# The last output tile of an attention and MoE kernel leaves by column halves instead of row halves

## The chip, the cores and the metric

The kernel runs on one core of a Trainium2 chip. A core has five engines that run their own instruction streams: TensorE (PE in the profile; its weight loads are listed apart as PEld), VectorE (DVE), ScalarE (ACT), GpSimd (POOL) and SyncE (SP), which here only issues transfers. Transfers are issued from SP and from ACT, and their packets are moved by the core's 16 DMA engines. The metric is device time in microseconds (us), lower is better. A time is given as the median of several runs. A profile is one further execution with its own time.

## The reference, cut to what matters

For each of 8 batches and 8 heads of 64 the reference computes a linear attention over 576 positions, brings the heads side by side (512 columns), and sends all 4608 rows through two matrices with a squared ReLU between them:

```python
kv = np.einsum('bhsd,bhse->bhde', k_s, v)        # k_s: softmax over positions
attn = np.einsum('bhsd,bhde->bhse', q_s, kv)     # q_s: softmax over the head's 64
x = attn.transpose(0, 2, 1, 3).reshape(B * S, H * D)   # 4608 x 512
h = x @ w_in                                     # 512 x 2048
g = s * np.maximum(h, 0.0) ** 2 + b
return g @ w_out                                 # 2048 x 512
```

All inputs and the output are float32. The output has 4608 rows of 512 columns; a batch owns 576 consecutive rows.

## The kernel before

Float32 products are made from pairs of float32r parts (a high and a low part), three matmuls for each product. TensorE runs nearly without a gap from start to end, and the rest is arranged around it.

The rows are cut into nine blocks of 512. Blocks 0 to 7 are the first 512 rows of each batch. The ninth block is made of what is left: 64 rows of each of the eight batches. Within a block the 2048 hidden columns are taken in 16 steps of 128. Each step makes `h` in PSUM (line 998), squares and splits it on ScalarE and VectorE, and adds its share to four output tiles of 128 x 512 (line 1061). For the ninth block the hidden part is made earlier, spread over the time of block 7, and the output part is done at the very end by `final(j)`, j = 0 to 3 (line 984): each makes one output tile of 128 rows by 512 columns from 16 x 3 matmuls, one tile after the other. Each tile has a PSUM bank of its own. Tile j holds the 64 left rows of batch 2j in partitions 0 to 63, and those of batch 2j+1 in partitions 64 to 127.

`leave_last(j)` takes such a tile out. It copies the whole PSUM bank into a slice of one SBUF tile named `last` (line 1088), by VectorE for j = 2 and by ScalarE for the others, and then issues two transfers (line 1092). SP sends partitions 0 to 63 into the 64 rows of batch 2j, and ACT sends partitions 64 to 127 into the 64 rows of batch 2j+1. Each transfer has 64 rows of 2 KB, 128 KB in all. Both issues wait for the one copy.

The order of the instructions is found when the kernel is built, by a planner (`Order.run`): the work is a set of generators, each `yield Op(engine, cost, due, needs, ...)` asks for a place on an engine, and the code behind the yield is emitted when that place has been given. Each engine's stream is then fixed, and executes in that order. For j = 3 the requests of `leave_last` come after everything else that any engine does, so no planned work stands behind them. Semaphore waits between engines are put in by the framework, from the tiles that the instructions read and write. Behind the kernel's last instruction the framework puts a closing sequence (line 1248), in which SP waits for every transfer and all engines meet.

Of the kernel before, what the change touches and what calls it, by code (L numbers as in the profile page):

```python
# [25 lines left out]
def attention_moe(ctx: ExitStack, tc: tile.TileContext, q, k, v, w_in, w_out, s, b, out):  # L26
    nc = tc.nc
    B, H, S, D = q.shape
    DM, FF = w_in.shape
    DO = w_out.shape[1]  # L30
# [3 lines left out]
    NQ = 4  # L34
    LEFT = S - NQ * P
    NT = NQ + 1
    TB = NQ * P
# [950 lines left out]
    acc = {}  # L988
# [91 lines left out]
    def leave_last(j):  # L1080

        t = B * NFC + NFC * (j + 1)

        yield Op("DVE" if j == 2 else "ACT", 0.6, t, needs=[f"final {j}"])
        if not lasts:
            lasts.append(work.tile([P, AREA], F32, name="last", tag="area"))
        o = lasts[0][:, j * DO:(j + 1) * DO]
        (nc.vector.tensor_copy if j == 2 else nc.scalar.copy)(o, acc[B, j])  # L1088
        for i, (e, eng) in enumerate((("SP", nc.sync), ("ACT", nc.scalar))):
            yield Op(e, 0.1, t)  # L1090
            bb = 2 * j + i
            eng.dma_start(out[bb * S + TB:(bb + 1) * S, :], o[half[i]])
# [116 lines left out]
    with tc.manual_schedule(engines={E.PE, E.DVE, E.Activation, E.Pool, E.SP}):  # L1209
        order.run(  # L1210
            [others(), transfers(), scalars()] + [fetch(f) for f in range(NFE, NFC)]
            + [x for pr in range(NP // 2, NP) for x in reload(pr)]
            + [conv_w(0, slice(i, i + 1)) for i in range(2)] + [conv_w(f, slice(0, 2)) for f in range(1, NFC)]
            + [k_stream(u) for u in range(NP)] + [k_pair(pr) for pr in range(NP // 2, NP)]
            + [q_stream(u) for u in range(2 * NP)]
            + [kv_stream(pr) for pr in range(NP // 2)] + [kv_second(pr) for pr in range(NP // 2, NP)]
            + [step(t) for t in range(NSTEP - 2 * NFC)]
            + [x for pr in late for x in reload_late(pr)] + [k_late(pr) for pr in late]
            + [k_exps(u) for u in range(2 * NP, NU)] + [q_late(u) for u in range(2 * NP, NU)] + [between()] + [kv_late(pr) for pr in late] + [x_late(u) for u in range(2 * NP, NU)]
            + [leave(blk, j) for blk in range(B) for j in range(2)] + [leave_last(j) for j in range(NQ)] + [left_over()]  # L1220
            + operands() + [sums(i) for i in range(HP)] + [late_pe()] + [quadrant(p, n) for p in range(HP) for n in range(4)] + [final(j) for j in range(NQ)]
        )
# [30 lines left out]
```

## Time and profile before

| what | value |
|---|---|
| median of 3 runs | 859.88 us (859.0 to 860.23) |
| the profiled execution's own time | 860.12 us |
| its span, first to last instruction | 858.2 us |
| time outside the span (860.12 - 858.2) | 1.9 us |
| PE busy | 846.7 us, 99% of the span |
| DVE busy | 590.8 us, 69% |
| ACT busy | 435.7 us, 51% |
| the four final tiles, 192 matmuls of line 984 | 43.7 us busy |
| granted TensorE clock | 1.000 |

A busy share close to 100% says which engine carries most of the span, not what sets the very end of it. The end is read from the timeline and from the transfer views of the last microseconds. In a transfer view a packet is one piece that a DMA engine moves; a queue's row gives its packets, the MB, and the time that the packets took as a share of 16 engines over the window. A row of issues gives the count, the KB of each transfer and the microseconds from its issue until it has landed. q1 carries what SP issues, q10 what ACT issues.

### The profile page before, as it was taken

The numbers are of one execution on the slowest core, as the hardware profiler recorded it, in microseconds if no ns is written. First come the engines' busy times: TensorE is split into PE (matmuls) and PEld (weight loads), VectorE is DVE, ScalarE is ACT, GpSimd is POOL, SyncE is SP. The second block draws the span as 40 slices with busy tenths as digits, with TensorE's granted clock in tenths as the row PEclk, the third lists the DMA queues.
The fourth block names the chain that finished last, engine by engine and source line by source line (L and its number), as shares of the span: only waits on it lengthen the run. The fifth ranks groups of instructions, "written<-read, shape, count | busy, mean of one in ns | idle before, by whom it ended". The sixth has DMA issues, their size and how long they took to land.

```text
span 858.2 us, 11838 instructions
## 1 busy us (share of the span) xinstructions
PE 846.7 (99%) x4406; PEld 699.5 (82%) x4406; DVE 590.8 (69%) x922; ACT 435.7 (51%) x733; POOL 164.4 (19%) x184
## 2 busy tenths in 40 slices
PE   8899999999999999999999999999999999999997
PEld 6688888888888888888888888888888888888886
DVE  6999976778685857777587867685766587656300
ACT  5898744446364535454544454454336665555300
POOL 1000011111121110211020202120023436665000
PEclk9999999999999999999999999999999999999999
DMA  9994134334333324333424314421530110000100
GB/s 262 303 379 145 34 87 138 83 94 104 115 85 86 84 89 132 90 83 89 132 77 97 90 68 93 123 61 50 132 90 1 53 50 0 1 1 1 49 25 25
DMA packets 106573, 79.47 MB, mean 93 GB/s; under 512 B 56212, under 2 KB 100244, under 8 KB 106388
## 3 DMA queue, kind: packets, MB, share of 16 engines
q1 hardware_dynamic: 105364, 77.60, 32.4%
q10 hardware_dynamic: 1152, 1.11, 0.4%
q8 instruction: 35, 0.57, 0.3%
q14 instruction: 22, 0.18, 0.1%
HBM read 60.29 MB, written 18.40 MB: 92 GB/s over the span
## 4 chain that ended last, share of the span: by engine, by line
PE 94%; DMA 3%; DVE 1%; ACT 1%; issue 0%; SPq 0%; ACTq 0%
PE acc L1061 41%; PE h L998 35%; PE q L875 8%; PE last L984 5%; PE kv L311 2%; PE qa L875 1%; DMA st<-in_moe_w_out_dram 1%; DMA raw<-in_q_dram 1%; PE xp L690 1%; PE xq L690 1%; DMA area<-in_q_dram 1%; PE xp L454 0%; DVE low L232 0%; PE qT L444 0%; DVE w L239 0%
## 5 line engine op out<-in xcount | busy, mean ns | idle before, releaser
L998 PE MATMUL h<-x,w 128*128 128x512 f32 x1344 | 329.5, 391 | 0.8 <-DVE x L463 0.8
L1061 PE MATMUL acc<-w,gh 128*128 128x512 f32 x1024 | 317.7, 391 | 0.0
L998 PEld LDWEIGHTS h<-x,w 128*128 128x128 f32 x1344 | 250.1, 188 | 53.2 <-DVE x L463 1.4
L1061 PEld LDWEIGHTS acc<-w,gh 128*128 128x128 f32 x1024 | 190.9, 188 | 39.4
L1061 PE MATMUL acc<-w,gl 128*128 128x512 f32 x512 | 199.6, 390 | 0.1
L1023 ACT ACTIVATE r<-h 128x512 f32<-128x512 f32 x112 | 66.8, 596 | 170.8 <-PE h L998 168.3
L1036 DVE SCALAR_TENSOR_TENSOR r<-r,sb 128x512 f32<-128x512 f32 x106 | 84.5, 798 | 92.2 <-ACT r L1023 91.7
L1061 PEld LDWEIGHTS acc<-w,gl 128*128 128x128 f32 x512 | 96.1, 188 | 20.6 <-DVE gl L1040 0.5
L1038 ACT ACTIVATE gh<-r,sb 128x512 fp32r<-128x512 f32 x106 | 76.7, 724 | 53.8 <-DVE r L1036 52.9
L1040 DVE SCALAR_TENSOR_TENSOR gl<-r,sb,gh 128x512 fp32r<-128x512 f32 x106 | 83.2, 785 | 29.5 <-ACT gh L1038 28.6
L589 POOL TENSOR_TENSOR area<-area,qm 128x640 f32<-128x640 f32 x24 | 33.5, 1399 | 134.8 <-DVE qm L587 119.4
L606 POOL TENSOR_TENSOR qe<-qe,qr 128x640 f32<-128x640 f32 x24 | 32.3, 1348 | 75.9 <-DVE qr L602 41.1
L984 PE MATMUL last<-w 128*128 128x512 f32 x192 | 43.7, 389 | 0.0
L984 PEld LDWEIGHTS last<-w 128*128 128x128 f32 x192 | 36.1, 188 | 7.5
L670 POOL TENSOR_TENSOR spare<-kvf,spare 128x256 fp32r<-128x256 f32 x12 | 9.8, 820 | 129.9 <-issue 119.4
L696 ACT COPY y<-xp 64x320 f32<-64x320 f32 x48 | 20.2, 420 | 26.9 <-PE xp L690 26.5
L576 ACT ACTIVATE area<-area 128x640 f32<-128x640 f32 x24 | 17.6, 737 | 18.7 <-DVE area L538 18.7
L578 POOL MEMSET area<- 64x128 f32 x24 | 4.8, 200 | 116.2 <-issue 92.4
L958 DVE SCALAR_TENSOR_TENSOR gl<-r,sb,gh 128x512 fp32r<-128x512 f32 x16 | 13.7, 855 | 17.1 <-ACT gh L953 17.1
L700 DVE TENSOR_TENSOR y<-xp,y 64x320 f32<-64x320 f32 x48 | 23.4, 488 | 2.7 <-ACT y L696 1.7
L1088 DVE COPY last<-last 128x512 f32<-128x512 f32 x1 | 0.7, 692 | 34.6 <-PE last L984 34.6
L311 PEld LDWEIGHTS kv<-area 128*64 128x64 f32 x600 | 18.7, 137 | 5.1 <-issue 3.3
(190 smaller groups left out, 1073.4 us busy)
## 6 DMA issues: line engine op xcount, KB each, us to landing
st<-in_moe_w_in_dram SPq DMA_DIRECT2D x16, 512.0 KB, 8.3
st<-in_moe_w_out_dram SPq DMA_DIRECT2D x16, 512.0 KB, 9.0
out_dram<-o SPq DMA_DIRECT2D x16, 512.0 KB, 2.6
turned<-area SPq DMA_DIRECT2D x24, 320.0 KB, 2.3
qT<-turned SPq DMA_DIRECT2D x48, 160.0 KB, 3.1
area<-in_q_dram SPq DMA_DIRECT2D x14, 512.0 KB, 5.4
area<-in_k_dram SPq DMA_DIRECT2D x14, 512.0 KB, 4.3
area<-in_v_dram SPq DMA_DIRECT2D x56, 128.0 KB, 5.0
```

What stands on the lines that cost most here:

```text
L311: nc.tensor.matmul(kv[h * D:(h + 1) * D, i], kt[:, i, h, n], vt(2 * i + h, n), start=(n == 0), stop=(n == NT - 1))
L589: nc.gpsimd.tensor_tensor(out=qt, in0=qt, in1=bc(qm, [P, 2, NT, D]), op=ALU.subtract)
L606: nc.gpsimd.tensor_tensor(out=qe_, in0=qe_, in1=qr, op=ALU.mult)
L700: nc.vector.tensor_tensor(out=y[half[h], at], in0=parts[h][a][half[h]], in1=y[half[h], at], op=ALU.add)
L875: nc.tensor.matmul(BANK[where], w(a)[:, c * P:(c + 1) * P], xs[b_][:, c], start=k in (0, 1, 3) and n == 0, stop=n == 5, skip_group_check=True)
L984: nc.tensor.matmul(t_, g[:, js], w_, start=(f == 0 and i == 0), stop=(f == NFC - 1 and i == 2))
L998: nc.tensor.matmul(hp_, w[:, j, c, :], x[:, c, :], start=(c == 0 and i == 0), stop=(c == NP - 1 and i == 2))
L1023: nc.scalar.activation(r, hp_, AF.Relu)
L1036: nc.vector.scalar_tensor_tensor(out=r, in0=r, scalar=s_col, in1=r, op0=ALU.mult, op1=ALU.mult)
L1038: nc.scalar.activation(gh, r, AF.Identity, bias=b_col)
L1040: nc.vector.scalar_tensor_tensor(out=gl, in0=r, scalar=b_col, in1=gh.bitcast(F32), op0=ALU.add, op1=ALU.subtract)
L1061: nc.tensor.matmul(acc[blk, j // 2][:, j % 2], g[:, js], w_, start=(f == 0 and i == 0), stop=(f == NFC - 1 and i == 2))
```

## The change

Only tile j = 3, the last one, is treated in another way. Its bank is read by two engines, each for one half of the columns and all 128 partitions: ScalarE copies columns 0 to 255 and ACT sends them; VectorE copies columns 256 to 511 and SP sends them. The two transfers still carry 128 KB each, now as 128 rows of 1 KB. The destination of each is a view of the output with three dimensions, 2 batches by 64 rows by 256 columns, and the source is 128 partitions by 256 columns. The code emits ScalarE's copy, ACT's issue, VectorE's copy and SP's issue, in this order. Tiles 0 to 2 leave as before.

```diff
         o = lasts[0][:, j * DO:(j + 1) * DO]
+        if j == NQ - 1:
+            rows = out.rearrange("(b s) e -> b s e", b=B)[2 * j:2 * j + 2, TB:S]
+            for e, eng, copy, es in (
+                ("ACT", nc.scalar, nc.scalar.copy, slice(0, DO // 2)), ("SP", nc.sync, nc.vector.tensor_copy, slice(DO // 2, DO))
+            ):
+                copy(o[:, es], acc[B, j][:, es])
+                yield Op(e, 0.1, t)
+                eng.dma_start(rows[:, :, es], o[:, es])
+            return
         (nc.vector.tensor_copy if j == 2 else nc.scalar.copy)(o, acc[B, j])
         for i, (e, eng) in enumerate((("SP", nc.sync), ("ACT", nc.scalar))):
```

## The prediction

> **What bounds the kernel now.** I read the page first, for the span and the chain of waits that ended last, and then the last microseconds.
>
> ```profile
> span 858.2 us, 11838 instructions
> PE 846.7 (99%) x4406; PEld 699.5 (82%) x4406; DVE 590.8 (69%) x922; ACT 435.7 (51%) x733; POOL 164.4 (19%) x184
> PE 94%; DMA 3%; DVE 1%; ACT 1%; issue 0%; SPq 0%; ACTq 0%
> ```
>
> TensorE carries the span, and the change doesn't touch its work. What can move is only what follows the last matmul. The chain in order of time from 853 us on (start, length, what), and the timeline of the same window, show that piece:
>
> ```profile
> 852.97 0.69 PE last L984 x3
> 853.66 0.02 issue
> 853.68 0.58 ACT last L1088
> ```
>
> ```profile
> 853.68 0.58 ACT L1088 COPY last<-last 128x512 f32<-128x512 f32 x1 [21.17 <-PE last L984]
> 854.29 0.47 SPq L1092 DMA_DIRECT2D out_dram<-last  x1
> 854.30 0.50 ACTq L1092 DMA_DIRECT2D out_dram<-last  x1
> ```
>
> The last matmul ends at 853.66, the copy runs from 853.68 to 854.26, and both transfers are issued 0.03 later. No engine computes after that; SP's waits show what the closing sequence waits for:
>
> ```profile
> SPq L1248 <- DMA out_dram<-last: 2.1, 2, 1.8
> ```
>
> So the end is set by the later of the two landings. The transfer view of the window 854.2 to 858.2 (40 slices of 0.1 us in its first row) shows both:
>
> ```profile
> DMA  0000000000007999495998400000000000000000
> GB/s 0 0 0 0 0 0 0 0 0 0 0 0 184 246 184 266 82 225 123 349 471 328 164 0 0 0 0 0 0 0 0 0 0 0 0 0 0 0 0 0
> DMA packets 160, 0.26 MB, mean 66 GB/s; under 512 B 32, under 2 KB 32, under 8 KB 160
> q1 hardware_dynamic: 80, 0.13, 16.3%
> q10 hardware_dynamic: 80, 0.13, 8.6%
> out_dram<-last SPq DMA_DIRECT2D x1, 128.0 KB, 2.3
> ```
>
> In this window ACT's transfer stands without a landing time; the window 843.5 to 846.2, with the same pair for the tile before, has it:
>
> ```profile
> out_dram<-last ACTq DMA_DIRECT2D x1, 128.0 KB, 2.6
> ```
>
> Packets run from slice 12, 855.4, so 1.1 us after the issue, to slice 22, about 856.5. The later landing is ACT's: 854.30 + 2.6 = 856.9, which is 0.4 after the last packets. From there to the end of the span are 858.2 - 856.9 = 1.3 us of closing. The tail is then 0.6 copy and hop, 1.1 start, 1.1 packets, 0.4 report, 1.3 closing.
>
> The same view tells how a transfer is shared out. 160 packets with 32 under 512 B are 2 x 64 rows of 2 KB and 2 x 16 small packets, one report from each of 16 engines: a transfer whose outermost dimension counts 64 uses all 16. Packet times: q10 took 8.6% of 16 x 4.0 us = 5.5 us for 64 rows, 86 ns for 2 KB on one engine; q1 16.3%, 10.4 us, 163 ns.
>
> **The change, part by part.** *The copies.* Copies of half the width stand in the groups by form, for other PSUM tiles:
>
> ```profile
> L696 ACT COPY y<-xq 64x256 f32<-64x256 f32 x48 | 17.6, 367 | 0.9
> L700 DVE TENSOR_TENSOR y<-xq,y 64x256 f32<-64x256 f32 x48 | 20.3, 422 | 1.0
> L1088 DVE COPY last<-last 128x512 f32<-128x512 f32 x1 | 0.7, 692 | 34.6 <-PE last L984 34.6
> ```
>
> These have 64 partitions where the new copies have 128; 128x512 takes 0.58 on ACT, so partitions are not what a copy's time goes by, and 0.37 is my value for ACT. For DVE 0.42 is the nearest row, and 692 ns for twice the width bounds it above. ACT's half is therefore copied at 853.68 + 0.37 = 854.05 and issued at 854.08, 0.2 earlier than now.
>
> No row shows two engines reading one bank at the same time. If VectorE starts with ScalarE, it ends at 853.68 + 0.42 = 854.10; if it is made to wait for ScalarE's read, at 854.08 + 0.42 = 854.50, and SP's issue moves to 854.53, 0.24 later than now. I take the wait, since the two copies name the same tile and the code emits ScalarE's first. The Trainium skill, PSUM — Partial Sum Buffer, section on bank collisions, says that two engines on one bank and quadrant at once, reads included, are an error and have to be ordered by a semaphore; by it the second number holds, and no run here shows it. Behind VectorE's copy nothing is queued but the closing sequence, and only SP's issue waits for it.
>
> *The issues.* One on each of SP and ACT as before, 0.47 and 0.50 us, none moved past another. The change adds one DVE copy and takes no transfer away.
>
> *The transfers* are the large term. They keep 128 KB each, but get 128 rows of 1 KB, and their destination's outermost dimension counts 2 (the batches) where it counted 64. The trace has no transfer with 2 there. The rows on either side are the 64 of above (16 reports, all engines) and the one-row loads of `s` and `b`, outermost count 1:
>
> ```profile
> sb<-in_moe_s_dram SPq DMA_DIRECT2D x1, 0.0 KB
> sb<-in_moe_b_dram SPq DMA_DIRECT2D x1, 0.0 KB
> ```
>
> In the view of the whole span these are the only two rows with no landing time. I read that as reports missing: a landing is found from a transfer's reports, and a one-row transfer has no work for sixteen engines. So a transfer can run on fewer, and its shape decides. A count of 2 is far nearer to 1 than to 64, and I take it that such a transfer is dealt out in two shares, one for each batch, to two engines.
>
> The Trainium skill, DMA: Bandwidth & Descriptors, section "Why a DMA increments its semaphore by 16 and not by 1", has this as a rule: the number of engines is the largest up to 16 that divides the slowest dimension of both sides, and a hardware queue takes the lowest-numbered ones. Here that is the common divisor of 2 and 128, two engines, the same two for both queues; the 16 reports for 64 rows agree with it, and by it the sum is the one below.
>
> The price of a 1 KB row on one engine: rows of 1280 B from SBUF to DRAM, alone on the engines, stand in the window 133.7 to 136.0:
>
> ```profile
> DMA packets 272, 0.33 MB, mean 142 GB/s; under 512 B 16, under 2 KB 272, under 8 KB 272
> q1 hardware_dynamic: 272, 0.33, 41.1%
> ```
>
> 41.1% of 16 x 2.3 us is 15.1 us for 256 rows (and 16 reports), 59 ns each; by bytes 47 ns for 1 KB. The 86 ns for 2 KB give 43, the 163 ns of q1 give 82. I take 47: those rows are the nearest in size and, as here, come from all 128 partitions.
>
> *The sum.* ACT issues at 854.08; first packets 1.1 later, 855.2. Each of the two engines moves 64 rows of ACT's and 64 of SP's, if both queues use the same two: 128 x 0.047 = 6.0 us, to 861.2. SP's rows come from 854.53 + 1.1 = 855.6 on, long before ACT's 64 (3.0 us) are through, so the wait of VectorE's copy costs nothing: ACT's packets hide it. Without that cover it would cost up to 0.4. Then 0.4 for the report and 1.3 closing: the span ends at 862.9, 4.7 later than 858.2. The profiled execution would take 860.12 + 4.7 = 864.8; it lies 0.24 above the median of the runs, 859.88, so I predict 864.6. All times below are on the median's basis. At 43 ns the packets take 5.5 us (864.1), at 59 ns 7.6 us (866.2).
>
> **The rivals.**
>
> *Sixteen engines after all.* The mechanism is that the rows are dealt by the 128 source partitions. Then the packets are as short as now: 128 rows of 1 KB on 16 engines are 8 x 47 = 0.4 us for each transfer. ACT's half lands near 854.08 + 2.3 to 2.6 = 856.4 to 856.7, SP's at 854.53 + 2.3 to 2.6 = 856.8 to 857.1, against 856.9 now: -0.1 to +0.2 if VectorE waits, and about -0.2 if both copies run together. The time is 859.9, no slower than before. For it speaks that every transfer of 64 or 128 rows in this trace uses all engines; against it the one-row loads. This one decides if the outermost count of one side doesn't limit the shares. It also holds the case that the change doesn't do what it says: the copies then run one after the other, and what ACT's half gains SP's half loses.
>
> *Two engines, but another two for each queue.* SP's half starts at 855.6 and takes 64 x 0.047 = 3.0 us: 858.6, landed 859.0, span 860.3, +2.1: 862.0. For it: no row shows which engines a transfer of few shares gets. Against it: in the last pair now each queue has 16 reports, so the queues have no engines of their own.
>
> *Two engines at q1's rate.* SP's rows now take 163 ns for 2 KB, and ACT's 86. If the slow rate belongs to the destination or to writes that come first, all rows run at 82 ns: 855.2 + 10.5 + 0.4 + 1.3 = 867.4, +9.2: 869.1. For it: the 163 ns stand beside the 86 ns in one window and on the same engines. Against it: 256 rows of 1280 B ran at 59 ns from the same SBUF side.
>
> **How the numbers follow.** Two shared engines at 43 to 59 ns: 0.67, with a range of its own from 864.0 to 866.2. Sixteen engines: 0.17. Two engines for each queue apart: 0.08. The slow rate: 0.06. The remaining 0.02 is drift of the runs. A measurement of this kernel can tell about 0.2% from no change, 1.7 us, so the sixteen-engine case is "same" and the three others are slower: 0.81. Faster by 1.7 us has no mechanism: the only gain that the rows allow is 0.2 us. I give it 0.02, same 0.17. The range runs from 861.9 (queues apart) to 869.1 (the slow rate) and leaves out 0.19.
>
> **What would show it.** In the last window of the profile after: 260 packets (256 rows and 2 x 2 reports) confirm two engines, 288 refute them. The busy digits of the DMA row should stand at 1 (2 of 16 is 0.125) for some 6 us at about 43 GB/s; 3 us, or a digit of 2, is the rival with queues apart. Digits as high as now, with the end near 858.2, refute the forecast. The ACT copy should take 0.37, with its issue at 854.08; the DVE copy should start about 0.4 after ScalarE's, or together with it if reads are not ordered. SP's closing wait for the last transfer should grow from 1.8 us to between 6 and 7. Everything up to 853.66 should stand within 0.2 us of now; if not, the difference doesn't come from the tail.

## The result and the profile after

The kernel after takes 864.85 us (median of 6 runs, 864.28 to 866.22) beside 859.75 us before (6 runs, 859.0 to 860.23): 5.1 us slower, a ratio of 1.0061 with a 95% interval of 1.0048 to 1.0074. The forecast was 864.6, slower.

The page's first line and the timeline of the last microseconds, as they stand after the change:

```profile
span 863.0 us, 11839 instructions
```

```profile
853.23 0.37 ACT L1093 COPY last<-last 128x256 f32<-128x256 f32 x1 [21.17 <-PE last L984]
853.63 1.08 ACTq L1095 DMA_DIRECT2D out_dram<-last  x1
853.63 0.42 DVE L1093 COPY last<-last 128x256 f32<-128x256 f32 x1 [10.59 <-ACT last L1093]
854.08 0.60 SPq L1095 DMA_DIRECT2D out_dram<-last  x1
```

The two copies don't run together: VectorE is released by ScalarE's copy and starts when that has ended. ACT's issue comes 0.4 us after the start of the copy, earlier than the 0.6 before the change; SP's comes 0.85 after it. The issue itself now occupies ACT for 1.08 us where it took 0.50.

From the start of the last copy to the end of the span it was 858.2 - 853.68 = 4.5 us before and is 863.0 - 853.23 = 9.8 us now. This stretch, called the tail below, holds the whole loss: 5.2 us in the profile, 5.1 in the medians. (The two spans differ by 4.8 us only, because the last copy started 0.45 us earlier in the profile after.) The transfer view of the window 854 to 863 (40 slices of 0.225 us), and SP's waits, show where it goes:

```profile
DMA  0000111111110111120111111111111100000000
DMA packets 260, 0.26 MB, mean 29 GB/s; under 512 B 4, under 2 KB 260, under 8 KB 260
q10 hardware_dynamic: 130, 0.13, 5.2%
q1 hardware_dynamic: 130, 0.13, 4.4%
```

```profile
SPq L1257 <- DMA out_dram<-last: 7.0, 1, 7.0
```

260 packets are 256 rows of 1 KB and only 4 reports, two for each transfer, where 64-row transfers had 16 each. The busy digit is 1 nearly throughout the 6.5 us in which rows move, 854.9 to 861.4: about an eighth of the engines. The packets' time is 9.6% of 16 x 9 us, 13.8 us, or 6.9 us on each of two engines, which fills that stretch (the times of successive packets overlap a little).

These figures alone would also fit a pair of engines for each queue, used one pair after the other. The window 858.3 to 858.8, in which both queues move rows, tells the two apart:

```profile
DMA packets 24, 0.02 MB, mean 49 GB/s; under 512 B 0, under 2 KB 24, under 8 KB 24
q1 hardware_dynamic: 12, 0.01, 6.9%
q10 hardware_dynamic: 12, 0.01, 6.9%
```

Each queue has half of the rows, and together they keep 13.8% of the 16 engines busy, where ACT's queue alone had 14.4% in the window 857.0 to 857.4 and SP's alone 14.0% in 859.5 to 860.2. Two pairs at that pace would have shown twice as much. So two engines, the same for both queues, moved everything, and SP waited 7.0 us for the last landing.

### The profile page after: what moved, and what is told of

The parts are those of the page before. It is cut to its first block, busy times and chain, and to the rows that moved or that the text cites. A ratio compares the mean times of both kernels' runs of the same rounds, so it can differ in the third digit from the quotient of the medians.

```text
span 863.0 us, 11839 instructions
## 1 busy us (share of the span) xinstructions
PE 846.6 (98%) x4406; PEld 700.0 (81%) x4406; DVE 590.9 (68%) x923; ACT 435.4 (50%) x733; POOL 164.3 (19%) x184
## 4 chain that ended last, share of the span: by engine, by line
PE 96%; DMA 1%; ACT 1%; DVE 1%; SPq 0%; ACTq 0%; issue 0%; DVEq 0%
PE acc L1061 41%; PE h L998 35%; PE q L875 8%; PE last L984 5%; PE kv L311 2%; PE qa L875 1%; PE xp L690 1%; PE xq L690 1%; DMA area<-in_q_dram 1%; PE xp L454 1%; PE kT L342 1%; DMA area<-in_v_dram 0%; PE qT L444 0%; SPq L297 0%; PE kn L355 0%; PE unused L1210 0%
```

## Experiments

Tails are read as above, from the start of the last copy to the end of the span; the expectations count from the last matmul, which ends some 0.03 us before. The time that stands beside a run's is that of the kernel before, measured with it. Where no interval stands, the profiled execution is the only run, and its tail decides, not its time.

### The same rows to a destination of one dimension

```diff
-                eng.dma_start(rows[:, :, es], o[:, es])
+                eng.dma_start(out[2 * j * S + TB:2 * j * S + TB + P, es], o[:, es])
```

> The kernel after, but each of the two transfers of the last tile goes to 128 consecutive rows of the output (rows 0 to 127 from the first left row of batch 6) instead of 64 rows of each of two batches: the destination's outermost dimension counts 128 instead of 2, the copies, the 128 rows of 1 KB, the queues and the bytes are the same. Its second half therefore lands in the wrong rows: it leaves out the left rows of batch 7 and overwrites the first rows of that batch. Theory (the outermost count of 2 confines each transfer to two DMA engines): sixteen engines again, 288 packets in the last window, from the last matmul to the end of the span 4.2 to 4.8 us as before the change (4.6) and not 9.8, time 859.3 to 860.3. Rival (rows of 1 KB, column halves with a stride, or the second copy are what is slow): the tail stays near 9.8 us and the time near 864.8.

859.32 us beside 859.52, ratio 0.9997 (0.9988 to 1.0007). Timeline, and transfer view of the window 853.4 to 857.4:

```profile
853.49 0.37 ACT L1093 COPY last<-last 128x256 f32<-128x256 f32 x1 [21.17 <-PE last L984]
853.89 0.37 ACTq L1095 DMA_DIRECT2D out_dram<-last  x1
854.35 0.34 SPq L1095 DMA_DIRECT2D out_dram<-last  x1
```

```profile
core 0 of [0], span 857.4 us
DMA  0000000000000289968998200000000000000000
DMA packets 288, 0.26 MB, mean 66 GB/s; under 512 B 32, under 2 KB 288, under 8 KB 288
```

The loss is gone with nothing changed but where the rows go. The same copies, the same wait of VectorE, the same 256 rows of 1 KB: 32 reports instead of 4, digits of 8 and 9, and all rows moved in 1.0 us where it took 6.5. The rival with 1 KB rows, the column stride or the second copy as the cause falls. The tail of 3.9 us is even below the 4.2 expected, and 0.6 below that of the kernel before: the issues take 0.34 to 0.37 us and the first packet follows 0.9 us after its issue, where the 64-row transfers of before took 0.47 to 0.50 and 1.1.

### Four transfers, one for each batch and half

```diff
-                yield Op(e, 0.1, t)
-                eng.dma_start(rows[:, :, es], o[:, es])
+                for i in range(2):
+                    yield Op(e, 0.1, t)
+                    eng.dma_start(rows[i, :, es], o[half[i], es])
```

> The kernel after, but each engine sends its column half in two transfers, one for each batch: 64 rows of 1 KB each, the output complete and right. Theory (outermost count): each of the four uses 16 engines, 320 packets in the last window. ACT issues 0.4 and about 0.9 us after the last matmul, SP 0.9 and about 1.4 after it; the last lands 2.3 to 2.6 later, 1.3 closing: tail 5.0 to 5.4 us, time 860.1 to 860.7. Rival (1 KB rows or column halves): the rows are the same, so the tail stays near 9.8 and the time near 864.8.

859.73 us beside 859.52, ratio 1.0 (0.999 to 1.0009). In the window 852 to 862:

```profile
DMA packets 321, 0.27 MB, mean 27 GB/s; under 512 B 64, under 2 KB 320, under 8 KB 320
```

256 rows and 4 x 16 reports (and one instruction fetch behind the end). The copy starts at 852.47 and the span is 857.2: a tail of 4.7, a little under the expected 5.0 to 5.4, and the time is below the expected 860.1 to 860.7 as well. So the very same rows reach the very same places in the time of the kernel before when the batch is not a dimension of the transfer.

### The two parts of the change apart

Only the copies: both engines copy a half, then the tile leaves as before.

```diff
+        if j == NQ - 1:
+            rows = out.rearrange("(b s) e -> b s e", b=B)[2 * j:2 * j + 2, TB:S]
+            nc.scalar.copy(o[:, 0:DO // 2], acc[B, j][:, 0:DO // 2])
+            nc.vector.tensor_copy(o[:, DO // 2:DO], acc[B, j][:, DO // 2:DO])
+            for i, (e, eng) in enumerate((("SP", nc.sync), ("ACT", nc.scalar))):
+                yield Op(e, 0.1, t)
+                eng.dma_start(rows[i], o[half[i]])
+            return
```

> Only the copies of the change: ScalarE and VectorE copy a column half each, and then the tile leaves in row halves of 64 x 2 KB, by SP and ACT as before. Theory: the copies run one after the other (0.38 and 0.42 us), both issues come 0.9 us after the last matmul where they came 0.65 before, tail 4.8 to 4.9 against 4.6 us: within the noise of the time. Rival (the second copy's wait is a main cost): the tail grows by more than 1 us.

Only the sends: one copy of the whole tile by ScalarE, then the two transfers of the change.

```diff
-                copy(o[:, es], acc[B, j][:, es])
+                if e == "ACT":
+                    copy(o, acc[B, j])
```

> Only the sends of the change: ScalarE copies the whole tile as before (0.58 us), then ACT and SP send the column halves to the destination with outermost count 2. Theory: both issues come 0.65 us after the last matmul, 260 packets, the tail is the 9.8 us of the change and 0.2 more for ACT's later issue: 9.9 to 10.2. If one transfer's rows wait until the other's have been given out, whichever queue is first, the second queue's first packet comes some 3 us after its issue here too; if the queues interleave when they are issued together, both start about 1.1 to 1.8 after it and the end is the same. Rival (the copies): tail 4.6.

The timeline of the copies alone, then that of the sends alone:

```profile
852.36 0.37 ACT L1090 COPY last<-last 128x256 f32<-128x256 f32 x1 [21.17 <-PE last L984]
852.76 0.42 DVE L1091 COPY last<-last 128x256 f32<-128x256 f32 x1 [10.59 <-ACT last L1090]
853.22 0.47 SPq L1094 DMA_DIRECT2D out_dram<-last  x1
```

```profile
853.69 0.59 ACT L1094 COPY last<-last 128x512 f32<-128x512 f32 x1 [21.17 <-PE last L984]
854.30 0.60 SPq L1096 DMA_DIRECT2D out_dram<-last  x1
854.31 1.33 ACTq L1096 DMA_DIRECT2D out_dram<-last  x1
```

The copies alone: span 857.1, tail 4.7, 0.2 more than before, which is their coming one after the other (its one run took 858.88 us, 0.3 below the fastest of the 19 runs of the kernel before beside it, so its time shows no cost). The sends alone: span 864.0, tail 10.3 and 865.82 us, the whole loss and 0.5 more, where 0.2 was expected for ACT's later issue. Rows began 1.2 us after the first issue in both kernels, so of the 0.5 some 0.2 is that first issue's later time (0.6 against 0.4 after the start of the copy), and the rest lies in the packets. Here SP issued first, by 0.01 us, and its rows came first: in the window 853.6 to 857.4 all 56 packets are SP's, so ACT's first row moved more than 3.0 us after its issue. Which queue comes late is not a matter of the queue or of VectorE's wait.

### Sixty-two rows, and sixty

The kernel before, with each queue's 64 rows of the last tile cut in two transfers, 62 and 2 rows, or 60 and 4:

```diff
-            eng.dma_start(out[bb * S + TB:(bb + 1) * S, :], o[half[i]])
+            cut = 62 if j == NQ - 1 else LEFT
+            eng.dma_start(out[bb * S + TB:bb * S + TB + cut, :], o[i * D:i * D + cut])
+            if cut < LEFT:
+                yield Op(e, 0.1, t)
+                eng.dma_start(out[bb * S + TB + cut:(bb + 1) * S, :], o[i * D + cut:(i + 1) * D])
```

> The kernel before (one copy by ScalarE, row halves of 2 KB rows by SP and ACT), but for the last tile each queue sends 62 of its 64 rows first and the other 2 rows in a transfer of their own. Theory, made sharper (a transfer is dealt over the largest number of engines up to 16 that divides its outermost count on both sides): 62 = 2 x 31 gives two engines, 31 rows of 2 KB on each for each queue at 86 ns: 2.7 us for one queue, 5.3 to 5.8 for both, and the tail is 8.5 to 9.5 us; 136 packets in the last window (124 rows + 4 rows + 4 x 2 reports); time 863.5 to 864.7. Rival (only a small outermost count confines, a count of 62 still spreads over all engines with uneven shares): the tail is that of before and 0.5 to 1.0 more for the second issues, 5.1 to 5.6; time 860 to 860.6.

> The same with 60 rows and 4 rows instead of 62 and 2. Theory (largest divisor up to 16): 60 gives 15 engines and 4 gives 4: 166 packets in the last window (128 rows, 2 x 15 and 2 x 4 reports), tail 5.1 to 5.8 us, the second issues being all that is added to before. Rival (any transfer that is not a multiple of 16 falls to few engines, or a second small transfer in each queue is itself the cost): the tail is that of the 62 rows, above 8 us.

62 rows: 865.09 us beside 859.47, ratio 1.0064 (1.0049 to 1.008). 60 rows: 859.52 in its one run. The transfer views of the window 852 to 862, first for 62, then for 60:

```profile
DMA  0000000000200101111010111111111111000000
DMA packets 136, 0.26 MB, mean 26 GB/s; under 512 B 8, under 2 KB 8, under 8 KB 136
q1 hardware_dynamic: 68, 0.13, 4.6%
```

```profile
DMA  0000000000497771000000010000000000000000
q1 hardware_dynamic: 83, 0.13, 6.1%
q10 hardware_dynamic: 83, 0.13, 3.5%
```

These two runs decide what the engines are counted by. With 62 rows a queue has 64 data packets and 4 reports, which fit 2 from the 62 rows and 2 from the 2 rows. With 60 it has 64 and 19, which fit 15 and 4. With two rows fewer in a transfer of whole 2 KB rows, without a third dimension, the span grows from 858.2 to 863.2; with two fewer again it is 857.6. It isn't the third dimension, a small count or a second small transfer: what fits every count of reports is the largest divisor up to 16 of the outermost count. The Trainium skill, DMA: Bandwidth & Descriptors, section "Why a DMA increments its semaphore by 16 and not by 1", states this rule, the largest number up to 16 that divides the slowest dimension of both sides; the reports here agree with it at 64 (16), 62 (2), 60 (15), 4 (4) and 2 (2).

The tails missed the expected figures both ways: 863.2 - 853.12 = 10.1 for 62 rows (8.5 to 9.5 expected, and 863.5 to 864.7 for the time: the digits of 0 show gaps in which not even two engines were busy), and 857.6 - 853.10 = 4.5 for 60 (5.1 to 5.8 expected: the second issues, about 0.3 us each, cost nothing).

### Only ACT's half on two engines

SP's half goes in two transfers of 64 rows, ACT's as in the change:

```diff
-                yield Op(e, 0.1, t)
-                eng.dma_start(rows[:, :, es], o[:, es])
+                for i in range(2 if e == "SP" else 0):
+                    yield Op(e, 0.1, t)
+                    eng.dma_start(rows[i, :, es], o[half[i], es])
+                if e == "ACT":
+                    yield Op(e, 0.1, t)
+                    eng.dma_start(rows[:, :, es], o[:, es])
```

> The kernel after, but only ACT's half goes to the destination with outermost count 2; SP sends its column half in two transfers of 64 rows of 1 KB, one for each batch, which by the earlier runs use all 16 engines. Question: why SP's first packet came 3.6 us after its issue in the kernel after (1.1 to 1.2 us elsewhere). Theory G (the rows of all queues are handed out one transfer after another, so a transfer whose two engines are full holds up the next, even where that one's engines are idle): SP's first packet comes 2.5 us or more after its issue. Theory E (only the two engines are full): SP's first packet, on one of the 14 idle engines, comes 1.0 to 1.6 us after its issue. Under both the tail is set by ACT's transfer or by the shares of SP's rows on the two engines: 7.8 to 9.0 us after the last matmul, against 4.6 before and 9.8 after; packets 130 on ACT's queue, 160 on SP's.

The question behind it: in the kernel after, SP issues at 854.08, and in the window 853.2 to 857.65 the transfer view has packets of ACT's queue and none of SP's:

```profile
DMA packets 94, 0.10 MB, mean 22 GB/s; under 512 B 0, under 2 KB 94, under 8 KB 94
q10 hardware_dynamic: 94, 0.10, 8.2%
```

So SP's first row moved 3.6 us after its issue. In the mixed kernel SP issues at 854.66, and its rows are there in the window 853.7 to 856.2:

```profile
854.66 1.11 SPq L1096 DMA_DIRECT2D out_dram<-last  x2
```

```profile
q1 hardware_dynamic: 8, 0.01, 5.8%
q10 hardware_dynamic: 28, 0.03, 4.1%
```

They came within 1.5 us while ACT's two engines were full, so a confined transfer doesn't hold up all others; theory G falls. The tail is 861.4 - 853.80 = 7.6, just under the expected 7.8 (863.27 us in one run). But E isn't enough either: if the two engines only took turns between the queues, SP's rows would have mixed with ACT's from the start in the kernel after. They do mix once they have begun, 12 and 12 in the half microsecond shown in the section on the result. What puts the start of a second transfer for the same two engines 3 us behind stays open.

### One half alone, and one queue for both

> The kernel after without SP's transfer: the right half of the last tile's columns is copied and not sent (it is left out of the output). ACT's transfer of 128 rows of 1 KB to the destination with outermost count 2 is alone. Question: in the kernel after, the first 2.5 us of ACT's rows came at 62 ns a row on each engine, later rows at 42. If the slow beginning belongs to a transfer's own start: 64 rows on each engine take 3.5 to 4.0 us, tail 6.9 to 7.4 us after the last matmul. If it comes from SP's transfer, issued 0.45 us later, or from its handing out: 64 x 42 to 47 ns, 2.7 to 3.0 us, tail 6.1 to 6.4 us. Packets in the last window: 130. If the rows were on sixteen engines: tail below 4.

> The kernel after, but SP issues both column halves, ScalarE's first; ACT only copies. Question: whether the two queues' sharing of two engines costs or spares anything. If the two engines' total work is all that counts (256 rows of 1 KB on two engines): the tail is that of the change, 9.3 to 10.2 us. If the two queues had engines of their own in part, the tail would be above 10.5. If the late start of the second queue (3.6 us after its issue) were a loss, one queue would do without it and end at 64 + 64 rows x 47 ns, tail 9.0 to 9.3.

```diff
+                if e == "SP":
+                    return
                 yield Op(e, 0.1, t)
                 eng.dma_start(rows[:, :, es], o[:, es])
```

```diff
-                yield Op(e, 0.1, t)
-                eng.dma_start(rows[:, :, es], o[:, es])
+                yield Op("SP", 0.1, t)
+                nc.sync.dma_start(rows[:, :, es], o[:, es])
```

Transfer views, window 852 to 862, of the half alone and then of the one queue:

```profile
DMA  0000000000001111111111111000000010000000
GB/s 0 0 0 0 0 0 0 0 0 0 0 8 25 37 45 25 41 37 16 37 49 49 49 45 49 12 0 0 0 0 0 0 33 0 0 0 0 0 0 0
```

```profile
DMA  0000000000010111111111111111111111110000
q1 hardware_dynamic: 260, 0.26, 8.4%
```

The half alone has a tail of 859.9 - 853.34 = 6.6 us (861.73 us in one run), between the two bands that were expected. Its rows start slowly with no second transfer there: some 30 GB/s over the first 2 us, 49 GB/s after (two engines at 42 ns for 1 KB each). So the slow beginning doesn't come from a second transfer; what it comes from stays open. The second half adds 9.8 - 6.6 = 3.2 us for its 64 rows on each engine, 50 ns a row. One queue for both gives 862.7 - 853.23 = 9.5 us (864.51 us in one run): the late start of the second queue costs no more than 0.3 us by these two profiles, since the two engines are full anyway, and dividing the work between two queues bought nothing.

### The change with an outermost count of 16

The g parts of the ninth block, high (by ScalarE) and low (by VectorE), are written in the order row, batch, so that each tile holds 16 left rows of all eight batches, and tiles 0 to 2 leave in one transfer each. The diff is cut to the high part and the view of the output:

```diff
-            nc.scalar.activation(gh, r, AF.Identity, bias=b_col)
+            by = (lambda x, p: x.rearrange(p, b=B, r=LEFT)) if last else (lambda x, p: x)
+            nc.scalar.activation(by(gh, "p (r b) -> p b r"), by(r, "p (b r) -> p b r"), AF.Identity, bias=b_col)
...
+        rows = out.rearrange("(b s) e -> s b e", b=B)[TB + P // B * j:TB + P // B * (j + 1)]
```

> The change with an outermost count that fills the engines, the output complete and right: the columns of the two g parts of the ninth block are written in the order row, batch instead of batch, row (by the access patterns of the ScalarE and VectorE instructions that write them), so that tile j holds 16 left rows of all eight batches and its destination is 16 rows by 8 batches by 512 columns. Tiles 0 to 2 leave in one transfer from SP, the last in column halves as in the change. Theory: sixteen engines, 288 packets in the last window; issues 0.4 and 0.9 us after the last matmul, SP's half lands 1.8 to 2.4 us after its issue, 1.3 closing: tail 3.9 to 4.6 us, that is 0.0 to 0.7 below before; time 858.9 to 859.6 beside 859.5 of before, at the edge of what can be told. Rival (a destination of two outer dimensions is itself slow, whatever its count): tail above 8 us, time near 864.8. If the reordered writes of the g parts are slow and TensorE waits for them, PE's end moves later while the tail stays short.

860.01 us beside 859.47, ratio 1.0008 (0.9999 to 1.0017). Transfer view, window 852 to 862, and the instructions that write the reordered high part, here and in the kernel before:

```profile
q10 hardware_dynamic: 144, 0.13, 5.1%
q1 hardware_dynamic: 144, 0.13, 4.2%
```

```profile
L954 ACT ACTIVATE w<-misc,sb x16: 1273/1287/1337, 698.9 to 807.7; 128x512 fp32r<-128x512 f32 x16
```

```profile
L953 ACT ACTIVATE w<-misc,sb x16: 714/723/727, 699.1 to 806.7; 128x512 fp32r<-128x512 f32 x16
```

A destination of two outer dimensions is fine when the outer one counts 16: 16 reports in each queue, and a tail of 858.5 - 854.18 = 4.3 us, 0.2 below the kernel before. The time, expected at 858.9 to 859.6, shows no gain. The scattered writes take 1.29 us where they took 0.72, and the last copy starts later than in any other profile here; that the one causes the other is argued, not shown. No version was measurably faster than the kernel before.

## Why the prediction was right, point by point

**The two engines** carried the forecast, and the packet count (260), the digit of 1 and the plain destination's run confirm them; that both queues share them is shown by the window in which their rows alternate. The argument from the trace was weaker than the result. It held that a count of 2 is nearer to 1 than to 64, but 62 is near 64 and gives two engines: the mechanism is the divisor. And it read the missing landing times of the one-row loads as few reports. That sign doesn't hold: ACT's transfers of the last tile stand without a landing time too, with 16 reports in the kernel before and in the run with the plain destination. From those rows alone, two engines would have been a lucky choice.

**The terms of the sum.** Copy on ACT 0.37 (0.37 predicted). VectorE's copy waits for ScalarE's and takes 0.42 (both as predicted). The first packets came 1.2 us after the issue (1.1). All rows took 6.5 us (6.0): the price of a row, 47 ns by bytes from 1280 B rows, was near that of steady rows (42 to 46 ns) but left out the slow beginning; over the whole stretch it is 51 ns. That is the mis-sized term. The report and the closing together were 1.6 to 1.7 (0.4 + 1.3). Added up, the tail grew by 5.2 us where 4.7 was forecast. That the span of 863.0 all but meets the forecast 862.9 is luck: the last copy started 0.45 us earlier, which hides the difference.

**The step that failed** is the one that let SP's rows come "from 854.53 + 1.1 = 855.6 on" and share the engines with ACT's. They began after 857.65. The profile before shows already that the 1.1 us is the start of the first queue only. In its window 854.2 to 856.0 all packets are SP's, so ACT's first row came 1.7 us or more after its issue, with 16 engines:

```profile
DMA packets 58, 0.12 MB, mean 66 GB/s; under 512 B 0, under 2 KB 0, under 8 KB 58
q1 hardware_dynamic: 58, 0.12, 32.9%
```

In the kernel after, the wrong start cost next to nothing, for the reason given there: the engines were full with ACT's rows. So VectorE's wait was indeed hidden, and the 0.2 that it costs without that cover is what the copies alone show.

**Sixteen engines.** The price of this rival, 859.9, fits the plain destination (859.32 beside 859.52) and the four transfers. Its tail was put at -0.1 to +0.2 of before; the plain destination's is 0.6 shorter, and its transfers of all 128 partitions were issued (0.34 to 0.37 us against 0.47 to 0.50) and started (0.9 against 1.1) faster than those of 64.

**The queues apart and the slow rate.** The first falls by the 13.8% of the window in which both queues move rows; the sum of the packet times alone wouldn't refute it, since it is the same whoever moves them. The second falls by the steady pace, 42 ns a row on each engine and not 82.

**What was to stand still.** The last copy was to start within 0.2 us of before; it started 0.45 earlier. Over all the profiles here it lies between 852.36 and 854.18, with the same matmuls ahead of it, so the bound was too narrow.

## What to carry to other kernels

Before a tile is sent, look at the outermost dimension of both sides of the transfer as it is issued: in every run here, the largest number up to 16 that divides both counts fits the number of DMA engines that moved it. The small count stood on the destination or on both sides; no run has it on the source alone. A view with a batch of 2 in front, or 62 rows, costs 5 to 6 us for 256 KB here, while one transfer for each batch, or a count that 16 divides, costs what it did before (60 rows, on 15 engines by the reports, cost no more). It matters most for the last transfer of a kernel, where nothing covers it; and splitting a copy by columns between two engines gained nothing here, because the second reader of the PSUM bank waited for the first.

## What the runs showed that was not expected

The issues changed in length, and the runs don't show by what. ACT's issue of the transfer with a count of 2 took 1.08 to 1.33 us and SP's 0.60, where the 64-row transfers took 0.47 to 0.50 and a plain transfer of 128 rows 0.34 to 0.37. But the 62-row transfers, on two engines too, were issued in 0.27 us by SP and 0.59 by ACT, so two engines alone don't make an issue long. The first row of the second transfer came 3 us or more after its issue when both shared the two engines, and within 1.5 us when it went to all sixteen. And rows of the 128-partition transfers ran faster than those of 64 partitions, for a reason that no run here shows: at 9.8 to 10.0% of 16 x 4 us, 6.3 us of packets for 128 rows, 50 ns for 1 KB with the plain destination, while the 64-row transfers of the same 1 KB rows took

```profile
q1 hardware_dynamic: 160, 0.13, 6.0%
```

6.0% of 16 x 10 us for 128 rows, 75 ns each (window 852 to 862 of the kernel with four transfers).
